# One written order for every operation, casting loads of GpSimd, and seven products from batch 2 on, in a fused attention and MLP kernel

## The chip, the cores and the metric

The kernel runs on one core of one Trainium2 chip. That core has five engines with a queue of instructions each: PE (TensorE, the matmuls), DVE (VectorE), ACT (ScalarE), POOL (GpSimd) and SP (SyncE, which here only issues DMAs), and 16 DMA engines that move data between HBM and SBUF. The metric is device time in microseconds: the median of several runs of the whole kernel. The kernel before takes **267.36 us** (median of 3 runs, 267.06 to 268.97).

## The reference

Two kernels are fused: an attention by landmarks (the Nystroem method), and behind it a layer norm with a two-layer MLP and a residual. There are 8 batches, 8 heads, 576 rows and 64 columns a head, so the MLP sees 8 x 576 rows of 512, with 2048 hidden columns.

```python
m, scale = 32, 1/sqrt(64)
q_lm, k_lm = means of 18 neighbouring rows of q and k      # 32 landmarks each
A  = softmax(scale * q    @ k_lm.T)      # 576 x 32
Bm = softmax(scale * q_lm @ k_lm.T)      # 32 x 32
C  = softmax(scale * q_lm @ k.T)         # 32 x 576
Z  = Bm.T / (norm1(Bm) * norminf(Bm) + 1e-06)
for _ in range(6):
    Z = 2 * Z - Z @ Bm @ Z               # towards the inverse of Bm
x  = A @ Z @ C @ v                       # heads side by side: 576 x 512 a batch
xn = (x - mean(x)) / sqrt(var(x) + 1e-06) * g_ln
out = x + relu(xn @ w_ch1) @ w_ch2       # w_ch1 512 x 2048, w_ch2 2048 x 512
```

Everything comes and goes as fp32. On the chip the matmuls take fp16.

## The kernel before, in words

**Stages of a batch.** The q, k and v of a batch come in six loads (two of each, four heads in one) of 128 partitions by 1152 fp32. Each lands in a staging tile (`stg`), from which another engine makes an fp16 copy: `nat` for q and k, `natv` for v. PE turns q and k (`TR`, L308), sums give the landmarks, small 32-wide matmuls do the six rounds on Z for all heads of a set of batches at once (sets are (1), (2), (3, 4), (5, 6), (7); batch 0 has its own code), and the products of exponentials (`ea`) with `m` give x, transposed for the MLP and in rows for the residual. The first layer of a batch is 16 chunks of 128 hidden columns, 16 matmuls' worth of K in four; its ReLU (`psh` to `hT`, fp16) is done by ACT or DVE. The second layer multiplies blocks of 128 rows of `hT` (4 blocks for an even batch, 5 for an odd one, which takes half a block along from the even one) with W2: 16 matmuls of 128x512 into one PSUM bank. DVE scales the bank by 1/std of the row and adds it to x (`xblk`), and the block is stored.

**Seven products.** From batch `FAST = 4` on, the first four blocks of a second layer (512 rows by 2048 by 512) are computed as a 2 x 2 by 2 x 2 product with seven products of quarter blocks instead of eight. Each of the seven is 16 matmuls of 128x256. The price is sums and differences of blocks: four mixes of W2 (`w2mix`, once for all batches, done by POOL in pieces of 128x512) and, for each batch, four mixes of hidden blocks in two pieces of 128x1024 each (`mix`, all on DVE), and 14 adds of 128x256 from PSUM into x instead of 4 of 128x512. The mixed blocks live in the ring of staging tiles.

**Weights.** W1 comes in 8 loads of 512 KB, is scaled by `g` on the way to fp16, and from batch 2 on is used in a form with its column mean taken away. W2 comes in 8 loads of 512 KB to staging tiles and is cast by POOL (`load_w2` L451, `cast_w2`). The instructions of the start stand in this order on their queues: batch 0's loads, W1's loads with POOL's scalings, four loads of batch 1 with their casts, then W2's loads with their casts, the last two loads of batch 1 among them.

```python
for i in range(8):
    if i == 3:
        for _ in range(2):
            b1.next_load()
            b1.next_cast()
    load_w2(i)
    cast_w2(i)
```

**What sets the order.** Every instruction on every engine is issued through `keep`, which fixes its place in the engine's queue; the place is chosen while the kernel is being built. A small planner (`Clock`) keeps for each engine an estimate of when it is free and for each tile of when it is written. Five streams of work (attention, totals, first layers, the first rows, second layers) offer their next operation with the time at which it could start, and the first that is ready by the estimate goes next; `help_out` puts loads, casts, mixes and stores between them when the engine they need is estimated to be free; a table (`AFTER`) holds some back until others have gone. Where nothing is ready, PE is given one matmul on zeros (`warm(1, 256)`, 20 such fillers with those of the start, of the form 128x256); and 27 matmuls of 128x160 on zeros stand ahead of everything. Tiles come from rings: a new one waits until the oldest of its ring has been read.

All loads and nearly all stores are issued by SP. All mixes of hidden blocks are on DVE. Casts of q and k are split: POOL 21, ACT 7, DVE 4 (32 loads).

Lines in the profile's rows: L298 is the helper through which DVE, ACT and POOL issue, L304 the matmuls, L308 the turns, L313 the loads of q, k and v, L451 those of W2.

Of the kernel before, what the change touches and what calls it, by code (L numbers as in the profile page):

```python
# [16 lines left out]
P = 128  # L17


@with_exitstack  # L20
def kernel(
# [16 lines left out]
    NGRP = NBLK // 4  # L38
# [10 lines left out]

    scale_qk = 1.0 / (D ** 0.5)  # L50
# [4 lines left out]
    nc.scalar.add_instruction(mybir.InstLoadActFuncSet(  # L55
        name=nc.get_next_instruction_name(), act_func_set_id=6, ins=[], outs=[]))

    const = ctx.enter_context(tc.tile_pool(name="const", bufs=1))
    wpool = ctx.enter_context(tc.tile_pool(name="wpool", bufs=1))


    NEVER = 1e12

    def name_of(x):
        return x.tensor.name if hasattr(x, "tensor") else x.name

    parted, mixed_, parted_w1 = {}, set(), set()

    def key_of(ap):

        return keys_of(ap)[0]

    def keys_of(ap):
        n = name_of(ap)
        if n not in parted:
            return [n]
        at = [ap.offset]
        for step, k in list(ap.ap)[1:]:
            if step >= parted[n]:
                at = [o + step * i for o in at for i in range(k)]  # L80
        if n in mixed_:
            return [f"{n}:{o // parted[n]}:{int(o % parted[n] >= 256)}" for o in at]
        return [f"{n}:{o // parted[n]}" for o in at]

    class Clock:


        WAY = 55.0
        OVERLAP = {"Activation": 110, "DVE": 80, "Pool": 30}

        def __init__(self):
            self.free = dict.fromkeys(("PE", "DVE", "Activation", "Pool", "SP"), 0.0)
            self.wrote, self.used, self.begun = {}, {}, {}
            self.small, self.lanes, self.wire = False, {}, 0.0
            self.cells, self.count, self.mark, self.fetched, self.ahead = [], 0, 95, 0.0, 0.0
            self.loads, self.pool = [], []
            self.free['PE'], self.issued = 1500.0, 0

        def share(self, span=3400.0):

            now = self.now()
            return sum(c for t, c in self.cells if t > now - span) / span

        def now(self):
            return max([self.free["PE"]] + list(self.lanes.values()))

        BLOCK, LEAD = 128, 16

        def both(self, *at):
            return max(max(at), ps2.next("p2", 2))  # L110

        def calm(self, n):

            return self.fetched if self.count + n + (20 if late() else 0) >= self.mark else 0.0

        def at(self, *tiles):
            return max([self.wrote.get(name_of(t), (0.0, ""))[0] for t in tiles] + [0.0]) + self.WAY

        def at_key(self, ap):
            return self.wrote.get(key_of(ap), (0.0, ""))[0] + self.WAY  # L120

        def idle_key(self, ap):
            n = key_of(ap)
            return max(self.wrote.get(n, (0.0, ''))[0], self.used.get(n, (0.0, ''))[0]) + self.WAY

        def idle(self, *tiles):

            return max([max(self.wrote.get(n, (0.0, ""))[0], self.used.get(n, (0.0, ""))[0],
                            self.begun.get(n, 0.0)) for n in map(name_of, tiles)] + [0.0]) + self.WAY

        def took(self, i, e, n, m):
            op = type(i).__name__
            if e == "Activation":
                return 300 if n < 8 else 190 + (1.07 if name_of(i.outs[0].bass_ap).startswith("ec_") else 0.79) * n
            if e == "Pool":
                if n == 1024 and name_of(i.outs[0].bass_ap) in mixed_:
                    return 2080
                if "Ptr" in op:
                    return 100 + 1.29 * n
                return 100 + 0.92 * n if "Copy" in op else 280 + 1.76 * n  # L140
            if n == 1152 and "Copy" in op:
                return 760
            if "Stats" in op:
                return 690 if m > 100 else 180
            if n >= 512 and (n == 576 or op == 'InstTensorCopy'):
                return 100 + 1.13 * n
            if n == 1024:
                last = max([b for a, b in self.pool if a <= self.ready < b] + [0.0])
                queued = 1000 if self.free["Pool"] > self.ready else 690
                return max(queued, last - self.ready + 560)  # L150
            if n == 256 and "Ptr" in op and name_of(i.outs[0].bass_ap).startswith("xblk"):
                return 480
            if "Transpose" in op:
                return 110 + 1.15 * n
            return 140 + 1.15 * max(n, m if "Reduce" in op else 0)

        def note(self, i):
            e = str(i.engine).rsplit(".", 1)[-1]
            outs = [a.bass_ap for a in i.outs if hasattr(a, "bass_ap")]
            ins = [a.bass_ap for a in i.ins if hasattr(a, "bass_ap")]  # L160
            size = [[k for _, k in a.ap] for a in outs + ins]
            count = []
            for dims in size:
                n = 1
                for k in dims[1:]:
                    n *= k
                count.append(n)
            reads = [n for a in ins for n in keys_of(a)]
            writes = [n for a in outs for n in keys_of(a)]
            ready = 0.0  # L170
            for n in reads:
                t, who = self.wrote.get(n, (0.0, e))
                if who != e or e != "PE":
                    ready = max(ready, t + (self.WAY if who != e else 0.0))
            for n in writes:
                for t, who in (self.wrote.get(n, (0.0, e)), self.used.get(n, (0.0, e)),
                               (self.begun.get(n, 0.0), "")):
                    if who != e:
                        ready = max(ready, t + self.WAY)
            if type(i).__name__ == "InstDMACopy":  # L180
                start = max(self.free[e], ready)
                self.free[e] = start + (580 if e == "SP" else 100)
                half_ = size[0][0] == 64 and any(n.startswith("stg") for n in writes)
                self.wire = (max(start + 1650, self.wire)
                             + count[0] * size[0][0] * 4 / (150.0 if half_ else 385.0))
                self.loads = self.loads[-24:] + [(start, self.wire)]
                self.issued += 1
# [3 lines left out]
            elif e == "PE":  # L191
                cols = count[0]
                if self.count == self.mark - self.LEAD:
                    self.ahead = self.now()
# [1603 lines left out]
```

## Time and profile before

| | before |
|---|---|
| median of the runs | 267.36 us (267.06 to 268.97) |
| span of the profiled execution, first to last instruction | 266.1 us |
| PE busy | 256.5 us, 96%, 3442 matmuls |
| DVE busy | 202.8 us, 76% |
| ACT busy | 175.2 us, 66% |
| POOL busy | 133.6 us, 50% |
| TensorE clock granted, mean | 0.999 |
| DMA moved | 46.68 MB, mean 175 GB/s |

The profiled execution is one run apart from the three that give the median; its span is 1.2 us below that median. "Busy" is the time in which an engine runs an instruction; the waits in between are named by what ended them. A group of rows in the list of costly instructions has the line, engine, operation, output and inputs, the shapes, the count, then the sum and the mean of one, then the idle time ahead of them by cause.

### The profile page before, as it was taken

To read this page: it belongs to the slowest core of one execution; us is meant where nothing else is said; L and a number is where in the kernel's file an instruction comes from. 1 tells how busy PE (TensorE), PEld (TensorE's weight loads), DVE (VectorE), ACT (ScalarE), POOL (GpSimd) and SP (SyncE) were. 2 spreads that over 40 slices of the span, in tenths; PEclk is the share of its full clock that TensorE was granted. 3 is DMA by queue.
4 is the path that set the end of the run, shared out by engine and by line. 5 is a ranking of instruction groups with operands and counts; after the bars stand their busy time and mean duration, and the time that the engine had idled before them with its cause. 6 is when DMAs were issued, how large, how long until landed. Compare 5 with 4: busy or idle time off the path is not lost.

```text
span 266.1 us, 8332 instructions
## 1 busy us (share of the span) xinstructions
PE 256.5 (96%) x3442; PEld 167.9 (63%) x3442; DVE 202.8 (76%) x461; ACT 175.2 (66%) x337; POOL 133.6 (50%) x160
## 2 busy tenths in 40 slices
PE   7889998999999999999999999999999999999994
PEld 7644754466545554546655465578878765788883
DVE  2657873899999979788984986989684599819762
ACT  2578997378868896589797559787377654871000
POOL 5288788999729387499999934500000042000000
PEclk9999999999999999999999999999999999999999
DMA  7999999999976996766611120110060006100606
GB/s 253 380 396 389 388 386 393 317 343 306 354 237 172 388 363 187 207 174 198 200 43 39 34 52 2 42 43 0 2 158 0 2 4 160 43 0 2 158 17 183
DMA packets 23566, 46.68 MB, mean 175 GB/s; under 512 B 2404, under 2 KB 2664, under 8 KB 23528
## 3 DMA queue, kind: packets, MB, share of 16 engines
q1 hardware_dynamic: 23048, 45.49, 53.3%
q10 hardware_dynamic: 480, 0.66, 0.7%
q8 instruction: 27, 0.44, 0.7%
q14 instruction: 11, 0.09, 0.1%
HBM read 36.70 MB, written 9.44 MB: 173 GB/s over the span
## 4 chain that ended last, share of the span: by engine, by line
PE 78%; DMA 11%; DVE 3%; POOL 3%; issue 2%; SPq 1%; ACT 1%; POOLq 0%; DVEq 0%
PE bank L304 51%; PE psh L304 21%; DMA stg<-in_v_dram 6%; DMA wstg<-in_moe_w_ch_dram 3%; DMA stg<-in_q_dram 2%; PE pscv L304 1%; POOL natv L298 1%; PE psd L304 1%; DVE xblk L298 1%; PE psec L304 1%; PE psm L304 1%; PE psea L304 1%; POOL w L298 1%; SPq L313 1%; DVE st L298 1%
## 5 line engine op out<-in xcount | busy, mean ns | idle before, releaser
L304 PE MATMUL bank<-w,hT 128*128 128x512 f16 (+3 forms) x528 | 111.7, 335 | 1.2 <-issue 0.8
L298 ACT ACTIVATE hT<-psh 128x576 f16<-128x576 f32 x119 | 73.6, 654 | 21.9 <-PE psh L304 21.0
L304 PEld LDWEIGHTS <-hT 128*128 128x128 f16 x656 | 60.3, 98 | 32.5 <-issue 8.6
L304 PE MATMUL psh<-ea,m 128*128 128x288 f16 x512 | 78.3, 286 | 0.6 <-DVE ea L298 0.3
L304 PEld LDWEIGHTS <-m 128*128 128x128 f16 x512 | 48.8, 97 | 20.2 <-issue 3.7
L298 DVE SCALAR_TENSOR_TENSOR xblk<-bank,rstd,xblk 128x256 f32<-128x256 f32 (+2 forms) x77 | 39.0, 539 | 22.4 <-PE bank L304 22.3
L298 POOL TENSOR_TENSOR ea<-ea,lns 128x576 f16<-128x576 f16 x14 | 18.9, 1371 | 60.4 <-ACT lns L298 54.6
L298 POOL CAST nat<-stg 128x1152 f16<-128x1152 f32 x21 | 23.8, 1147 | 8.5 <-DVE xT L298 6.4
L298 DVE BATCH_NORM_STATS2 six<-xblk 128x6 f32<-128x512 f32 x36 | 24.2, 673 | 0.9 <-ACT xblk L298 0.9
L298 POOL CAST natv<-stg 128x1152 f16<-128x1152 f32 (+1 forms) x17 | 19.3, 1165 | 9.7 <-DMA stg<-in_v_dram 7.7
L298 DVE STREAM_TRANSPOSE xT<-nat 128x576 uint32<-128x576 uint32 x28 | 21.4, 763 | 0.0
L298 ACT COPY xblk<-bank 128x512 f32<-128x512 f32 (+1 forms) x32 | 18.0, 591 | 4.0 <-PE bank L304 3.7
L304 PE MATMUL bank<-w2mix 128*128 128x256 f16 x128 | 17.1, 273 | 0.0
L304 PE MATMUL bank<-w2mix,hT 128*128 128x256 f16 x128 | 15.8, 273 | 0.0
L298 DVE SCALAR_TENSOR_TENSOR st<-st,bank 128x128 f16<-128x128 f16 (+2 forms) x36 | 11.1, 308 | 5.9 <-PE bank L304 5.7
L298 ACT CAST m<-bank 128x512 f16<-128x512 f32 x18 | 9.9, 586 | 7.5 <-PE bank L304 7.4
L298 DVE TENSOR_REDUCE part<-xT 128x32 f16<-128x576 f16 x20 | 14.6, 744 | 0.2
L298 ACT ACTIVATE lns<-psd 128x576 f32<-128x576 f32 x16 | 10.3, 644 | 6.0 <-PE psd L304 5.9
L304 PE MATMUL bank<-zcbd,ea 128*128 128x256 f16 x80 | 14.1, 273 | 0.0
L298 DVE SCALAR_TENSOR_TENSOR m<-less,zsum,bank 128x512 f16<-128x512 f16 (+1 forms) x18 | 11.5, 682 | 3.0 <-PE bank L304 1.4
L304 PEld LDWEIGHTS <-w2mix 128*128 128x128 f16 x128 | 12.4, 98 | 2.0 <-issue 0.2
L304 PEld LDWEIGHTS <-st 32*32 32x32 f16 x448 | 5.9, 90 | 11.9 <-DVE st L298 8.9
(135 smaller groups left out, 365.9 us busy)
## 6 DMA issues: line engine op xcount, KB each, us to landing
stg<-in_q_dram SPq DMA_DIRECT2D x16, 576.0 KB, 6.3
stg<-in_k_dram SPq DMA_DIRECT2D x16, 576.0 KB, 6.0
out_dram<-xblk SPq DMA_DIRECT2D x66, 128.0 KB, 2.4
wstg<-in_moe_w_ch_dram SPq DMA_DIRECT2D x16, 512.0 KB, 7.3
stg<-in_v_dram SPq DMA_DIRECT2D x10, 576.0 KB, 7.2
stg<-in_v_dram SPq DMA_DIRECT2D x6, 288.0 KB, 6.2
stg<-in_v_dram SPq DMA_DIRECT2D x12, 144.0 KB, 6.0
out_dram<-xblk ACTq DMA_DIRECT2D x4, 128.0 KB, 3.2
```

Of the source, the lines that this page charges most:

```text
L298: return lambda *args, **kw: keep(getattr(self.engine, op)(*args, **kw))
L304: keep(nc.tensor.matmul(o, l, r, start=start, stop=stop, tile_position=(rb, cb), skip_group_check=(skip or cb != 0)))
L313: keep(queue.dma_start(out=t[:], in_=src[b, 4 * u:4 * u + 4].rearrange("(r e) (t j) d -> (e t) r j d", e=2, j=NJ)))
```

## The change

The planner goes. Every operation gets a name and a list of engines that may do it, and one string of 1585 entries gives the order in which all operations are issued, and the engine of each:

```diff
+ORDER = """
+0G 1S 11D 10P 15P 16A 2S 236G 12D 18P 3S 13G 17P 4S 21P 23P 27D 19A 14A 20P 26P 28D 29P 30A 51P 52A
...
+    names = list(OPS)
+    order = [(names[int(x[:-1])], x[-1]) for x in ORDER.split()] if ORDER else [(n, OPS[n][0][0]) for n in names]
+    for n, e in order:
+        emit(n, e)
```

`emit` takes a free buffer of the right kind for each tile that the operation is the first to use, and frees it after its last use, so buffers are no longer rings. The stages of a batch, the sets and the arithmetic of each stage stay.

W2 comes in four DMAs of 128x4x512 that GpSimd issues straight into the fp16 tile (the DMA casts); in the order the first of them stands behind the loads of q and k of batch 1, the other three behind those of batch 2 and behind GpSimd's two casts of v of batch 1.

```diff
-    def load_w2(i):
-        stg = stage.tile([P, 2, DM], FP32, name="wstg", tag="stg")
-        keep(nc.sync.dma_start(out=stg[:], in_=w2_src[:, ts(i, 2), :]))
-        w2_coming.append(stg)
-    def cast_w2(i):
-        pool.tensor_copy(out=w2_16[:, ts(i, 2), :], in_=w2_coming[i][:])
+        for i in range(4):
+            op(f"load_w2_{i}", "G", (),
+               lambda e, i=i: dma(e, w2_16[:, ts(i, 4), :], w2_src[:, ts(i, 4), :]))
```

q and k of batches 1 to 7 come likewise, in 14 DMAs of GpSimd into fp16 tiles with both halves of a batch in one (1.18 MB of fp32 read each). Batch 0's q and k, and all v, still come as fp32 and are cast by an engine.

The seven products start two batches earlier, and a mix of hidden blocks may go to GpSimd:

```diff
-    FAST = 4
+    FAST = 2
...
-    def mix(o, left, right, op, k):
-        n = ds(k, 4)
-        dve.tensor_tensor(out=o[:, n, :], in0=left[:, n, :], in1=right[:, n, :], op=op)
+                def mix(e, i=i, c=c):
+                    o, x, y = mixes[i][1]()
+                    tt(e, o[:, ds(c, 4), :], x[:, ds(c, 4), :], y[:, ds(c, 4), :], mixes[i][2])
+                op(f"hmix_{b}{i}{c}", "DG", uses, mix)
```

In the new order, 33 of the 48 mixes of hidden blocks are GpSimd's, 11 ReLUs go from ACT to DVE, some casts of v go from GpSimd to DVE and ACT, and 20 whole stores instead of 4 are issued by ACT. The fillers are gone but for the 27 matmuls at the very start:

```diff
-                if at[k] > now + 250 and clock.share() < 0.5 and banks.next() <= now:
-                    warm(1, 256)
-                    continue
...
-        if (w, nm) != (U - 1, "k"):
-            warm(3, 256)
```

More of the change, by code (lines that the diff above doesn't have):

```diff
@@ L1422 @@
+    HK, HN = MCH // 2, DM // 2
     w11, w12 = w2_16[:, 0:HK, 0:HN], w2_16[:, 0:HK, HN:DM]
     w21, w22 = w2_16[:, HK:MCH, 0:HN], w2_16[:, HK:MCH, HN:DM]
[L1425 to L1438 removed]
```

2330 lines of the change are left out of this document (908 added, 1422 removed), and 9 rows, old and new, of the table AFTER.

## The prediction

> **What bounds the kernel now.** I read the page's head first (who is busy, the clock, the chain that ended last), then four stretches of the span, then what TensorE itself waits for.
>
> ```profile
> span 266.1 us, 8332 instructions
> ...
> PE 256.5 (96%) x3442; PEld 167.9 (63%) x3442; DVE 202.8 (76%) x461; ACT 175.2 (66%) x337; POOL 133.6 (50%) x160
> ...
> PEclk9999999999999999999999999999999999999999
> ...
> PE 78%; DMA 11%; DVE 3%; POOL 3%; issue 2%; SPq 1%; ACT 1%; POOLq 0%; DVEq 0%
> ```
>
> ```profile
> 0.00:50.00 50.00, 45.11 (x706) 28.50 (x707) 31.12 (x89) 32.87 (x62) 36.40 (x61) 1.00 1.00 371
> 50.00:100.00 50.00, 50.00 (x635) 28.77 (x634) 46.46 (x100) 41.16 (x79) 37.20 (x42) 1.00 0.93 305
> 100.00:160.00 60.00, 59.09 (x943) 33.23 (x941) 49.55 (x110) 44.05 (x90) 48.93 (x51) 1.00 0.45 125
> 160.00:240.00 80.00, 79.76 (x960) 58.04 (x958) 58.69 (x130) 56.46 (x106) 11.02 (x8) 1.00 0.16 38
> ```
>
> ```profile
> PE bank L304 <- DVE zeros L340: 1.5, 1, 1.5
> ...
> PE bank L304 <- issue: 0.8, 1, 0.8
> PE bank L304 <- POOL w L298: 0.5, 1, 0.5
> ```
>
> The columns of the stretches are length, then busy time of PE, weight loads, DVE, ACT, POOL, then clock, DMA share, GB/s. Two kernels stand in one span. Up to 50 us the DMA engines are full (share 1.00 at 371 GB/s) and PE is idle for 50.00 - 45.11 = 4.9 us. From 50 to 240 us PE is idle for 0.00 + 0.91 + 0.24 = 1.15 us of 190. So behind the start almost nothing is left to win from a better order: the time falls by what PE no longer has to compute, or by an earlier start. Two more things are read from these rows: DVE is at 46.46 of 50 in the second stretch, and POOL is nearly idle (11.02 of 80) in the fourth.
>
> **The change part by part.** Counts of instructions are those of the two programs.
>
> *Seven products for batches 2 and 3.* Their eight blocks of 16 matmuls 128x512 become two times seven products of 16 matmuls 128x256.
>
> ```profile
> 99.61 1.47 PE L304 MATMUL bank<-w,hT 128*128 128x512 f16 x6
> 100.92 0.65 PE L304 MATMUL psh<-ea,m 128*128 128x288 f16 x4
> 101.41 0.22 PE L304 MATMUL bank<-st,bones 128*128 128x128 f16 x1
> ...
> 188.25 1.91 PE L304 MATMUL bank<-w2mix,hT 128*128 128x256 f16 x16
> 190.00 1.91 PE L304 MATMUL bank<-w,hT 128*128 128x256 f16 x16
> ```
>
> From start to start (a mean duration overlaps its neighbour), six wide matmuls take 100.92 - 99.61 = 1.31 us, 0.218 each; a whole product takes 1.75. Per batch: 64 x 0.218 = 13.95 before, 7 x 1.75 = 12.25 after. Two batches: **-3.4 us**, on the path, as PE has no idle time there. All other matmuls keep their number and form, but for 20 fillers (below).
>
> *What the seven products add on DVE and POOL.* The mixes of hidden blocks go from 32, all on DVE, to 48: 15 on DVE and 33 on POOL. The adds of 128x256 go from 56 to 84, those of 128x512 from 19 to 11.
>
> ```profile
> L298 POOL CAST nat<-stg 128x1152 f16<-128x1152 f32 x21 | 23.8, 1147 | 8.5 <-DVE xT L298 6.4 <-DMA stg<-in_k_dram 1.1 <-PE bank L304 0.4
> L298 POOL TENSOR_TENSOR w2mix<-w 128x512 f16<-128x512 f16 x8 | 9.0, 1151 | 0.0
> L298 POOL CAST w<-wstg 128x1024 f16<-128x1024 f32 x8 | 8.1, 1038 | 1.2 <-DMA wstg<-in_moe_w_ch_dram 0.7 <-PE psd L304 0.3
> ...
> L298 DVE SCALAR_TENSOR_TENSOR xblk<-bank,rstd,xblk 128x256 f32<-128x256 f32 x56 | 24.2, 476 | 20.4 <-PE bank L304 20.3
> L298 DVE SCALAR_TENSOR_TENSOR xblk<-bank,rstd,xblk 128x512 f32<-128x512 f32 x19 | 13.8, 731 | 0.0
> L298 DVE TENSOR_SCALAR hT<-psh 128x576 f16<-128x576 f32 x9 | 6.8, 754 | 1.0 <-PE psh L304 0.8
> L298 DVE TENSOR_TENSOR w2mix<-w2mix,hT 128x1024 f16<-128x1024 f16 x8 | 6.3, 792 | 0.0
> L298 DVE TENSOR_TENSOR hT<-hT 128x1024 f16<-128x1024 f16 x8 | 5.2, 683 | 0.0
> ...
> L298 ACT CAST nat<-stg 128x1152 f16<-128x1152 f32 x7 | 8.0, 1159 | 0.0
> ```
>
> No row shows POOL on a two-input mix of 1024. It lies between the 1.04 of a one-input cast of that size and twice the 1.15 of a mix of 512, 2.3; I take 2.1, near the double, because the mix is the same operation: 33 x 2.1 = 69 us of POOL. DVE: 17 mixes fewer at about 0.73 (-12.4), 28 adds of 0.476 more (+13.3), 8 adds of 0.731 fewer (-5.8), 11 relus taken from ACT (9 become 20; 11 x 0.754 = +8.3), and about 12 of small things (5 casts of v, copies of m, mixes of W2, scalings of W1). 202.8 + 15 = about **218 us**, 82% of the span instead of 76. ACT loses the 11 relus and 7 casts (8.0): about 160. All this is cover, not path, as long as PE never waits for it; what it costs if it does is the second rival.
>
> *Casting DMAs.* POOL loses 20 casts of q and k (22.9), the 8 of W2 (8.1) and about 18 us of casts of v, scalings and other operations given to DVE and ACT; it gains 18 DMA issues (14 of 1.18 MB for q and k, 4 of 1.05 MB for W2). The trace has no DMA issued by POOL. The nearest rows are SP's issue of a load half as large and what POOL does when it touches every element:
>
> ```profile
> 0.80 0.44 SPq L313 DMA_DIRECT2D stg<-in_q_dram  x1
> ...
> 37.38 2.36 POOL L298 CAST natv<-stg 64x1152 f16<-64x1152 f32 x2 [0.40 <-DMA stg<-in_v_dram]
> 39.80 3.99 POOL L298 CAST w<-wstg 128x1024 f16<-128x1024 f32 x4
> 44.08 1.04 POOL L298 CAST w<-wstg 128x1024 f16<-128x1024 f32 x1 [0.28 <-PE psd L304]
> ```
>
> One issue costs between 0.44 and 2.3 us (two casts of 1.15, its own share of elements); I take 0.9, two issues of SP, since it is an issue. 18 x 0.9 = 16. POOL then holds 133.6 - 49 + 69 + 16 = about **170 us** (bounds: 127 to 202), with the new mixes where the fourth stretch has it idle. Off the path in the sum.
>
> *The start.* It is DMA-bound, so bytes in order set it.
>
> ```profile
> stg<-in_q_dram SPq DMA_DIRECT2D x16, 576.0 KB, 6.3
> ...
> wstg<-in_moe_w_ch_dram SPq DMA_DIRECT2D x16, 512.0 KB, 7.3
> ```
>
> A batch's q, k and v are six loads of 0.59 MB, a weight eight of 0.52. Ahead of the last quarter of W2 the old order has 3.5 MB (batch 0), 4.2 (W1), 3.5 (batch 1) and W2's own 4.2, 15.5 MB: 41.7 us at 371 GB/s, and the trace has W2's last cast at 44.08 to 45.1. The new order puts q and k of batch 2 (2.36 MB) ahead, and the last three quarters of W2 stand on POOL's queue behind both casts of batch 1's v: 17.8 MB, 48 us, landing near 50. So W2 is complete about 5 us later. What covers it: 13 of batch 0's 16 first-layer chunks now stand ahead of its first second-layer matmul instead of 8, 5 chunks of 101.41 - 100.92 = 0.49, 2.5 us; left +2.5. Against it: POOL, which cast q, k, v and W2 one after another up to 45 us, is rid of 12 of these (12.8 us), and PE's 4.9 us of idle time there have something to shrink. I set -2.5 for that and **0** for the start, with ends of +7 (no cover) and -8 (all idle time and the fillers gone).
>
> *Fillers.* 20 matmuls on zeros go, 17 of them in five groups from the first to the last of these rows.
>
> ```profile
> L304 PE MATMUL bank<-zeros 128*128 128x256 f16 x20 | 3.3, 274 | 0.0
> ```
>
> ```profile
> 6.62 0.49 PE L304 MATMUL bank<-zeros 128*128 128x256 f16 x3
> ...
> 13.50 0.61 PE L304 MATMUL bank<-zeros 128*128 128x256 f16 x4
> ```
>
> They stand where PE would wait, so they are worth 0 in the sum; what kept warm by them is the third rival.
>
> *Order.* Of the 1.15 us of idle time behind 50 us I take half: **-0.6**. The stores go partly to ACT's queue (20 instead of 4 whole ones, 16 x 0.44 = 7 us of issuing on an engine at 66%): nothing. The SP queue loses 36 loads, and a load now waits behind fewer stores: nothing.
>
> The sum against the profiled execution: 266.1 - 3.4 + 0 - 0.6 = 262.1. The runs' median, 267.36, lies 1.2 over the span; so **263.3 us**, 1.5% faster.
>
> **Rivals.**
>
> *W2 late (slower).* Place: the first 50 us, where the DMA share is 1.00 and nothing is spare. Of the 17.8 MB, 8.9 are now cast on the way. If casting halves the rate of these bytes, they take 8.9 / 0.371 = 24 us more of the DMA engines; half of that lies beside first-layer work and batch 1's attention, 12 us do not: 266.1 - 3.4 + 12 - 0.6 + 1.2 = 275 us. It decides as soon as W2's last quarter lands after about 53 us. For it: W2 comes last, and its issue waits in POOL's queue behind casts that wait for v. Against: a casting load reads the same bytes and writes half.
>
> *DVE becomes the bound (no change).* DVE is at 93% in the second stretch already and gets 15 us more. If 3 to 5 us of it fall where PE waits for a bank, the gain is gone: 266.1 - 3.4 + 3.5 + 1.2 = 267.4. [...]
>
> *The clock (no change).* The clock was granted in full (1.00) in all stretches. Without fillers the front of batch 0 has gaps.
>
> ```profile
> L308 PE MATMUL pst<-ident,nat 128*128 128x128 f16 x36 | 3.1, 242 | 0.9 <-DVE nat L298 0.8
> ...
> L304 PE MATMUL bank<-pm,nat 128*128 128x64 f16 x36 | 1.7, 194 | 0.2 <-DVE nat L298 0.2
> ```
>
> At half the clock these would take twice as long: 266.1 - 3.4 - 0.6 + 4.8 + 1.2 = 268.1. [...]
>
> *A better start (faster still).* Half of the start's 8.2 us (4.9 idle, 3.3 fillers) goes: 266.1 - 3.4 - 0.6 - 4.1 + 1.2 = 259.2.
>
> **How the numbers follow.** The forecast 0.36 (its own range 260.5 to 264.6), the better start 0.14, DVE 0.26, the clock 0.05, W2 late 0.19. 1% of 267.36 is 2.7 us, about what a measurement of this kernel tells from no change; faster is below 264.7: 0.36 + 0.14 = 0.50. Within 1%: 0.26 + 0.05 = 0.31. Slower: 0.19. The range 257 to 271 takes in the first four cases and the light end of the last; what it leaves out is most of W2 late and the best of starts.
>
> **What would show it.** The seven products: 672 matmuls 128x256 of them at 1.75 us a product, and none of the wide ones in batches 2 and 3 but the fifth block's. The start: PE's idle time in 0 to 50 us (4.9 before), and the landing of the last W2 load (50 forecast). POOL: the mix of 1024 at 2.1 us, the issue at 0.9. DVE: busy 218, its mixes near 0.73 rather than over 1, and no wait of PE for DVE above 1 us in all behind 50 us. The clock: digits of 9 throughout. The forecast is wrong if PE's idle time behind 50 us rises above 4 us, or if PE is past 50 us with less done than before: the start is the term I know least.

## The result

The changed kernel takes **281.37 us** (median of 6 runs, 279.54 to 282.27) against 268.06 for the kernel before in the same runs: a ratio, estimated from the single runs, of 1.0479 (95% interval 1.042 to 1.0538). It is **4.8% slower**; forecast was 263.3, with a range of 257 to 271. Here and below, medians take in all runs, and ratios leave out the few that fell into a slower state of the chip.

### The profile after

The page's head, as it was read of the kernel before; the profiled execution is the fastest of the six, its span 11.7 us longer than the one before.

```profile
span 277.8 us, 8397 instructions
...
PE 256.3 (92%) x3518; PEld 179.6 (65%) x3518; DVE 221.4 (80%) x491; ACT 165.1 (59%) x316; POOL 169.3 (61%) x167
...
PEclk9956999999999999998999999999999999999997
...
PE 72%; DVE 17%; ACT 3%; DMA 2%; issue 2%; SPq 0%; ACTq 0%
```

Then the same four stretches (length, busy PE, weight loads, DVE, ACT, POOL, clock, DMA share, GB/s).

```profile
0.00:50.00 50.00, 41.68 (x664) 26.69 (x665) 34.34 (x94) 32.74 (x58) 30.13 (x60) 0.90 1.08 276
50.00:100.00 50.00, 46.71 (x560) 26.10 (x558) 47.96 (x95) 29.48 (x61) 31.48 (x34) 1.00 0.75 164
100.00:160.00 60.00, 57.07 (x1071) 41.37 (x1070) 55.89 (x125) 44.39 (x89) 49.36 (x45) 0.97 0.57 125
160.00:240.00 80.00, 79.06 (x937) 58.95 (x935) 59.74 (x129) 50.26 (x94) 42.98 (x24) 1.00 0.20 48
```

The engines' sums are as forecast: DVE 221 (218 forecast), POOL 169 (170), ACT 165 (160). What was not: PE is idle for 8.3 us up to 50 us (4.9 before) and for 3.29 + 2.93 + 0.94 = 7.2 us from 50 to 240 (1.15 before). DVE's share of the chain that ended last went from 3% to 17%. The clock's row has a 5 and a 6 near the start and an 8 in the middle. The two longest waits of PE behind the start (sum, times, longest):

```profile
PE it L192 <- DVE st L209: 3.1, 3, 2.3
PE psea L192 <- ACT lns L202: 2.5, 1, 2.5
```

To place the loss, TensorE's **useful work** is added up along the trace: each matmul on data counts with the time from its start to the next one's, but at most with the pace of its form where nothing waits, the median distance of two starts in the trace of the changed kernel (0.109 us for 256 columns, 0.123 for 288, 0.216 for 512; for the small tiles 0.06 is taken, where those of 128x128 start 0.056 apart). What is missing against the kernel before at the same moment is time lost so far.

| useful work done, us | by 20 | by 40 | by 60 | by 90 | by 120 | by 130 | by 190 | in all |
|---|---|---|---|---|---|---|---|---|
| before | 7.1 | 24.4 | 40.8 | 67.4 | 93.5 | 102.8 | 157.7 | 225.4 |
| changed | 5.9 | 18.9 | 36.8 | 60.4 | 87.2 | 92.4 | 145.3 | 223.1 |
| missing | 1.2 | 5.5 | 4.0 | 7.0 | 6.3 | 10.4 | 12.4 | |

So there is a loss at the start (5.5, of which 4.0 stay), one of 3.0 between 60 and 90 us and one of 4.1 between 120 and 130. Against it stand 2.3 us less work, the seven products. The last matmul is 9.2 us later than before, which leaves 0.4 net for the stretches in between. What is still missing lies behind it: the last operation of DVE ends 262.97 before and 272.20 now, the spans end 3.1 and 5.6 us later, 2.4 more. 4.0 + 3.0 + 4.1 + 0.4 - 2.3 + 2.4 = 11.6 of the 11.7.

The middle first. DVE, POOL, ACT and PE about 120 us (start, duration, and in brackets the idle time ahead and what ended it):

```profile
118.34 0.78 POOL L222 DMA_DIRECT2D nat_q<-in_q_dram  x1
118.55 4.44 DVE L206 TENSOR_TENSOR ea<-ea,lns 128x576 f16<-128x576 f16 x1
119.14 2.13 POOL L206 TENSOR_TENSOR hT<-hT 128x1024 f16<-128x1024 f16 x1
121.21 1.17 POOL L199 CAST natv<-stg_v 128x1152 f16<-128x1152 f32 x1
122.32 0.95 POOL L206 TENSOR_TENSOR s_q<-asum_q,nat_q 128x128 f16<-128x128 f32 x1
...
123.08 0.65 ACT L202 ACTIVATE lns<-psd 128x576 f32<-128x576 f32 x1 [3.56 <-DVE ea L206]
123.79 0.43 PE L192 MATMUL psea<-xT_q,lmt_k 32*32 32x288 f16 x20 [2.49 <-ACT lns L202]
```

One operation of DVE on operands in SBUF took 4.44 us; another of its form in this run took 0.75. POOL ran all that time with no gap between its instructions, and DVE was done 0.6 us after the third of them. No gap opened for it there either: POOL's fourth instruction, the sum `s_q`, began at once and took 0.95 us, where the ten of its form take 0.50 on average. ACT waited for DVE's result, PE for ACT's. The clock records then show half speed from 124.2 to 127.6 us. Between 60 and 90 us two more stand out:

```profile
64.00 0.78 POOL L222 DMA_DIRECT2D nat_q<-in_q_dram  x1 [1.40 <-DVE xT_k L219]
64.19 2.07 DVE L206 TENSOR_TENSOR mix<-w 128x512 f16<-128x512 f16 x1
64.80 1.17 POOL L206 TENSOR_TENSOR mix<-w 128x512 f16<-128x512 f16 x1
...
74.47 3.16 DVE L206 TENSOR_TENSOR w<-w,less 128x1024 f16<-128x1024 f16 x1
74.82 1.14 POOL L206 TENSOR_TENSOR mix<-w 128x512 f16<-128x512 f16 x1
75.93 1.15 POOL L206 TENSOR_TENSOR asum_q<-nat_q 128x512 f32<-128x512 f16 x1
77.16 1.06 POOL L206 TENSOR_TENSOR asum_q<-asum_q 128x256 f32<-128x256 f32 x1
...
80.67 0.24 PE L192 MATMUL it<-st 32*32 32x64 f16 x8 [2.31 <-DVE st L209]
```

The mix of 64.19 takes 2.07; the same form took 0.38 at 52.47 us. PE waits 0.9 us for what DVE does behind it. The operation of 74.47, which centres W1, ends at 77.63, just behind the first gap in POOL's row (77.08 to 77.16); its form takes 0.67 elsewhere. What DVE had to do behind it, a cast of v of 1.29 us among it, came late, and PE's rounds on Z waited 2.3 us.

The casting loads did what was forecast. Two rows of queues (packets, MB written, share of the 16 DMA engines' time in the span): that of the casting loads after the change, and that of the loads and stores before:

```profile
q0 software_dynamic: 9504, 10.36, 23.6%
```

```profile
q1 hardware_dynamic: 23048, 45.49, 53.3%
```

The row of the casting loads counts 10.36 MB written, which are 20.7 MB read as fp32: 23.6 / 20.7 = 1.14% per MB read, against 53.3 / 45.49 = 1.17% before. So the GB/s of the stretches (276 against 371) fall because half as much is written, not because the loads are slower. W2's last quarter landed at 50.0 us, the forecast's 50, and no wait of PE is for a DMA.

### The profile page after: what moved, and what is told of

Same layout as the page of the kernel before. It is cut to its first block, busy times and chain, and to the rows that moved or that the text cites. A ratio compares the mean times of both kernels' runs of the same rounds, so it can differ in the third digit from the quotient of the medians.

```text
span 277.8 us, 8397 instructions
## 1 busy us (share of the span) xinstructions
PE 256.3 (92%) x3518; PEld 179.6 (65%) x3518; DVE 221.4 (80%) x491; ACT 165.1 (59%) x316; POOL 169.3 (61%) x167
## 3 DMA queue, kind: packets, MB, share of 16 engines
q0 software_dynamic: 9504, 10.36, 23.6%
## 4 chain that ended last, share of the span: by engine, by line
PE 72%; DVE 17%; ACT 3%; DMA 2%; issue 2%; SPq 0%; ACTq 0%
PE psh L192 20%; PE ps7a L192 14%; PE pso L192 9%; PE ps7c L192 8%; PE ps7e L192 3%; PE psy L192 3%; PE psm L192 3%; PE it L192 3%; DMA stg_k<-in_k_dram 2%; DVE m L209 2%; PE pscv L192 2%; DVE m L199 2%; DVE ea L206 2%; DVE w L206 2%; PE psf L192 1%
## 5 line engine op out<-in xcount | busy, mean ns | idle before, releaser
L192 PEld LDWEIGHTS <-m 128*128 128x128 f16 x512 | 47.5, 98 | 20.7 <-issue 3.9
L192 PE MATMUL pso<-w,hT 128*128 128x512 f16 x176 | 44.1, 380 | 0.1
L206 POOL TENSOR_TENSOR mix<-hT 128x1024 f16<-128x1024 f16 x7 | 14.9, 2125 | 30.6 <-ACT hT L202 20.0
L206 POOL TENSOR_TENSOR ea<-ea,lns 128x576 f16<-128x576 f16 (+1 forms) x14 | 16.7, 1193 | 24.5 <-ACT lns L202 15.4
L209 DVE SCALAR_TENSOR_TENSOR x<-ps7a,rstd,x 128x256 f32<-128x256 f32 x48 | 21.4, 473 | 6.7 <-PE ps7a L192 6.5
L192 PE MATMUL ps7a<-mix,hT 128*128 128x256 f16 x192 | 25.7, 276 | 0.0
L206 POOL TENSOR_TENSOR mix<-mix,hT 128x1024 f16<-128x1024 f16 x10 | 21.5, 2156 | 6.3 <-DVE mix L206 5.9
L934 DVE BATCH_NORM_STATS2 six<-x 128x6 f32<-128x512 f32 x36 | 24.2, 672 | 0.0
L206 POOL TENSOR_TENSOR hT<-hT,mix 128x1024 f16<-128x1024 f16 x9 | 19.0, 2121 | 6.9 <-PE ps7e L192 6.9
L199 ACT CAST m<-psm 128x512 f16<-128x512 f32 x31 | 17.1, 592 | 9.7 <-PE psm L192 7.1
L1003 DVE TENSOR_SCALAR hT<-psh 128x576 f16<-128x576 f32 x20 | 14.9, 750 | 9.2 <-PE psh L192 8.9
L192 PEld LDWEIGHTS <-mix 128*128 128x128 f16 x192 | 18.6, 99 | 3.5 <-issue 0.6
L199 ACT COPY x<-psy 128x512 f32<-128x512 f32 (+1 forms) x33 | 19.2, 586 | 2.2 <-PE psy L192 1.8
L202 ACT ACTIVATE lns<-psd 128x576 f32<-128x576 f32 x16 | 10.4, 650 | 12.0 <-PE psd L192 6.6
## 6 DMA issues: line engine op xcount, KB each, us to landing
w1s<-in_moe_w_ch_dram SPq DMA_DIRECT2D x8, 512.0 KB, 11.6
```

Source lines behind the costliest of these rows:

```text
L192: keep(nc.tensor.matmul(o, l, r, start=start, stop=stop, tile_position=(rb, cb), skip_group_check=(skip or cb != 0)))
L199: keep(nc.scalar.copy(o, i) if e == "A" else ENGINES[e].tensor_copy(out=o, in_=i))
L202: keep(nc.scalar.activation(*args, **kw))
L206: keep(ENGINES[e].tensor_tensor(out=o, in0=a, in1=b, op=f))
L209: keep(ENGINES[e].scalar_tensor_tensor(out=o, in0=a, scalar=s, in1=b, op0=f0, op1=f1))
L934: keep(nc.vector.bn_stats(out=T(f"six_{j}")[:], in_=T(f"x_{j}")[:]))
```

## The experiments

All times are medians; the ratios are to the kernel before on the same chip.

| run | median, us | ratio, 95% interval | span |
|---|---|---|---|
| changed kernel | 281.37 | 1.0479 (1.042 to 1.0538) | 277.8 |
| fill | 281.80 | 1.0500 (1.0468 to 1.0532) | 280.1 |
| unblock | 275.82 | 1.0268 (1.0223 to 1.0313) | 274.2 |
| one_ea | 277.94 | 1.0373 (1.0293 to 1.0453) | 274.3 |
| tail | 278.12 | 1.0368 (1.0334 to 1.0402) | 276.9 |
| allthree (fill, unblock, tail) | 272.96 | 1.0194 (1.0135 to 1.0254) | 271.4 |
| two_edits (unblock, tail) | 273.43 | 1.0207 (1.0159 to 1.0255) | 271.0 |
| mixes_on_dve | 298.42 | 1.1120 (1.1066 to 1.1174) | 294.5 |
| eight_in_2_3 | 287.00 | 1.0727 (1.0666 to 1.0787) | 284.8 |
| start | 283.74 | 1.0600 (1.0568 to 1.0632) | 281.8 |
| start2 | 283.01 | 1.0532 (1.0475 to 1.0589) | 279.4 |
| start3 | 279.50 | 1.0433 (1.0390 to 1.0476) | 276.9 |
| before_no_fillers | 269.99 | 1.0089 (1.0059 to 1.0119) | 268.8 |
| before_five | 271.91 | 1.0129 (1.0088 to 1.0170) | 269.5 |
| before_b1_first | 279.79 | 1.0419 (1.0366 to 1.0472) | 278.3 |
| before_b1_both | 285.15 | 1.0647 (1.0611 to 1.0683) | 283.3 |

### The clock at the start: fill, two_edits, before_no_fillers

Run fill, the changed kernel with matmuls on zeros put back:

```diff
+    def fillers(i, n):
+        def go(e):
+            t = pools["bank"].tile([P, 512], FP32, name="idle", tag=f"bank{free['bank'][-1]}")
+            for _ in range(n):
+                MM(t[:, 0:256], zeros[:, 0:P], zeros[:, 0:256])
+        op(f"filler_{i}", "P", (), go)
+    for i, n in enumerate((4, 6, 1, 2, 4, 5, 2, 2, 3, 4, 3)):
+        fillers(i, n)
```

> The changed kernel with 36 matmuls 128x256 on zeros put back between batch 0's first operations (11 places, 3 to 16 us). Theory A (the lost start is the halved clock from 15.0 to 25.2 us, set off by TensorE's gaps before it): the clock stays at 1.00, the 8.5 us of busy time in that stretch shrink by about 4, and the span falls from 277.8 to 273 to 274.5. Rival (TensorE is late there because of the order of the operations and of the loads, and the slow clock only stretches waits): the clock recovers, the span falls by less than 1.5 us.

Measured: 281.80 us, no gain. The stretch from 10 to 20 us, and the next, first of the changed kernel, then of fill:

```profile
10.00:20.00 10.00, 7.07 (x133) 5.07 (x131) 6.55 (x20) 3.99 (x8) 2.45 (x3) 0.75 1.07 306
20.00:30.00 10.00, 8.40 (x156) 4.54 (x155) 7.05 (x18) 8.64 (x17) 5.09 (x8) 0.74 1.08 327
```

```profile
10.00:20.00 10.00, 8.22 (x166) 5.67 (x164) 5.92 (x20) 4.62 (x7) 2.02 (x3) 1.00 1.09 325
20.00:30.00 10.00, 7.94 (x172) 4.75 (x170) 7.55 (x19) 8.64 (x17) 4.69 (x7) 1.00 1.03 286
```

The clock is back at 1.00, and the useful work by 40 us is 18.5, not more than the 18.9 without fillers. Theory A is refuted: the clock does fall at the start, but bringing it back wins nothing there. The pair of allthree and two_edits, with and without the fillers, says the same (272.96 and 273.43; the latter at a clock of 0.55 from 10 to 20 us):

> The run with the three edits together, without its 36 fillers. If the clock that falls at the start without them costs nothing, because the steps there wait for each other and not for TensorE's speed: within 1.5 us of 272.96. If the halved clock costs what TensorE's busy time in it says: 275.5 or more.

In the kernel before, where PE has more to do at that time, taking the fillers away does cost:

```diff
         idle = banks.take([P, 512])
+        if cols == 256:
+            clock.free["PE"] = clock.now() + 110 * n
+            return
```

> The kernel before without its 20 fillers of 128x256 (the 27 matmuls at the very start stay). If gaps alone halve the clock at the start and this costs time: a stretch at 0.5 of 3.4 to 10.2 us within the first 30, and 2 to 5 us more. If the clock falls but the small dependent steps there don't wait for TensorE's speed, as the run with fillers suggests: less than 1.5 us more.

Measured: 2.2 us more, with 3.4 us at half clock from 15.9. So that is what the fillers were worth in the kernel before, where the forecast had them at 0; the changed kernel's start hangs on something else.

### DVE held off by POOL: unblock, one_ea, mixes_on_dve

In unblock five entries of the order change; 731 is the scaling of ea at 118.55, 578 the mix of hidden blocks beside it, 492 the centring at 74.47, 438 a cast of v, and 500 a mix of W2:

```diff
-500D
+500G
...
-492D
-438D
+438A
...
+492D
 493D
...
 1375G
-578G
 588D
...
 730A
+731G
+578G
 732P
...
 1043A
-731D
 1044S
```

> The changed kernel with four operations moved or given to another engine: the scaling of ea that took 4.44 us on DVE at 118.6 goes to POOL ahead of the mix beside it, the mix of W2 that took 2.07 on DVE at 64.2 goes to POOL, the centring of W1 that took 3.16 at 74.5 goes behind the rounds on Z, and one cast of v from DVE to ACT. Theory B (a DVE operation with only SBUF operands waits for a gap in a run of POOL instructions): TensorE's waits of 2.5 us at 121 and 2.3 at 78 go, and with the first the halved clock of 124.2 to 127.6 (1.7 us): the span falls by 5 to 6.5 us. Rival (DVE is simply full, the wait moves to the next DVE operation): it falls by less than 2.5.

This text takes the mix of W2 that was moved for the one of 64.19, but it is another: entry 500 is the mix that DVE did in 0.38 us at 52.47. The long one stayed on DVE and is as long in unblock:

```profile
66.21 2.07 DVE L206 TENSOR_TENSOR mix<-w 128x512 f16<-128x512 f16 x1
```

Measured: 275.82 us, **5.6 less**. PE's waits of 2.5 and 2.3 us are gone and the clock stays at 1.00 behind the start; the 0.9 us behind the long mix are still there. Counted as useful work, 2.1 us are won between 60 and 90 us and 3.6 between 90 and 130. The first part comes from two moves at once, the centring put behind the rounds on Z and the cast of v given to ACT; how much of it is owed to POOL and how much to the order alone was not separated. To see how much the one operation at 118.55 is worth, one_ea has only the moves of 731 and 578:

> The changed kernel with one operation moved: the scaling of ea that took 4.44 us on DVE at 118.6 goes to POOL, ahead of the mix of hidden blocks beside it. If DVE was held off by POOL's run of instructions: TensorE's wait of 2.5 us at 121 and the halved clock of 124.2 to 127.6 go, 3.5 to 4.5 us of the 5.5 that the four moves brought together. If DVE's load is the cause: less than 1.5.

Measured: 277.94 us, 3.4 less, just short of the 3.5 expected (2.8 less by the ratios; the runs lie between 276.0 and 281.1). The span is 3.5 shorter. Two stretches, first of the changed kernel, then of one_ea:

```profile
118.00:124.00 6.00, 3.51 (x77) 2.57 (x76) 6.00 (x6) 2.41 (x4) 5.25 (x5) 1.00 0.69 96
124.00:130.00 6.00, 6.00 (x136) 3.96 (x105) 4.93 (x13) 2.90 (x6) 5.16 (x4) 0.72 0.58 160
```

```profile
118.00:124.00 6.00, 6.00 (x152) 4.63 (x149) 4.88 (x12) 4.33 (x7) 5.98 (x6) 1.00 0.69 105
124.00:130.00 6.00, 5.96 (x70) 4.25 (x61) 5.75 (x12) 4.50 (x8) 6.00 (x6) 1.00 0.95 299
```

POOL is busier than before (11.98 of these 12 us, 10.41 before). DVE issues 24 operations instead of 19 in about the same busy time (10.63 us, 10.93 before), and PE has hardly any idle time: it was the meeting of one DVE operation with a run of POOL instructions, not DVE's load. Theory B holds for this operation, but for its gap: no gap in POOL's row let DVE go on. The opposite cure, all mixes back on DVE, shows what POOL's share was good for:

```diff
-575G 577G 576G
+575D 577D 576D
...
```

> The changed kernel with all 48 mixes of hidden blocks on DVE, one letter each in the order. DVE gets 33 x 0.69 = 23 us and loses the stretches that a busy POOL sets off. Theory B (DVE is held off by runs of POOL instructions): no DVE operation over 2.5 us is left behind 100 us, the wait of 2.5 us at 121 goes, and the span falls by 1 to 4 us. Rival (DVE's own amount of work is the bound): the span rises by 3 us or more.

Measured: 298.42 us, 17 more; the rival is right here. The meeting is gone, as theory B has it: the same scaling of ea, now at 123.25 us, takes 0.74. But PE's longest waits (sum, times, longest) are now for DVE's own work:

```profile
PE ps7a L192 <- DVE x L209: 5.2, 3, 3.6
PE it L192 <- DVE st L209: 3.5, 4, 2.3
```

### The end: tail, and the three together

In tail, batch 6's last two adds (1368, 1365) and its stores go ahead of batch 7's:

```diff
 1508D
+1368D
+1365D
+1359A
+1360S
+1357A
+1366S
+1369A
+1367S
+1370A
 1520D
```

> The changed kernel with the last two adds of batch 6 put ahead of batch 7's on DVE, and batch 6's stores ahead of batch 7's on the queues. Theory C (5.6 us pass behind the last matmul, 3.1 before, because the last stores queue behind others): the span falls by 1.5 to 2.5 us. Rival (the stores' landing takes that long anyway): less than 0.8.

Measured: 278.12 us, 3.2 less in the median. The store queue of SP, and DVE's last operation, first of the changed kernel, then of tail:

```profile
266.58 7.75 SPq L222 DMA_DIRECT2D out_dram<-x  x9
...
271.85 0.35 DVE L209 SCALAR_TENSOR_TENSOR x<-pso_74b,rstd,x 128x128 f32<-128x128 f32 x1 [0.28 <-PE pso_74b L192]
```

```profile
268.73 5.25 SPq L222 DMA_DIRECT2D out_dram<-x  x6
```

```profile
273.07 0.35 DVE L209 SCALAR_TENSOR_TENSOR x<-pso_74b,rstd,x 128x128 f32<-128x128 f32 x1 [0.28 <-PE pso_74b L192]
```

Behind DVE's last operation lie 276.9 - 273.42 = 3.5 us instead of 5.6: three stores less stood ahead of the last one. Theory C holds for these 2.1 us. DVE's last operation comes 1.2 later in the profiled run of tail, the slowest of its four, so that the two profiled spans differ by only 0.9; the 3.2 of the medians, more than the 1.5 to 2.5 expected, has an interval wide enough for 2.1.

> The edits of the three other runs together. If A, B and C hold and add up: 277.8 - 4 - 6 - 2 = 266 for the span, 267 to 270 as a median, the time of the kernel before. If the lost time only moves to other waits: 273 or more.

Measured: 272.96 us, 8.4 less: the 5.6 of unblock and the 3.2 of tail add up, fill adds nothing. So the time misses the 267 to 270 that were expected if all three theories held, by about the 4 us set down for theory A. The stretches of allthree:

```profile
0.00:50.00 50.00, 43.30 (x700) 28.11 (x701) 34.47 (x94) 32.55 (x58) 29.74 (x60) 1.00 1.05 270
50.00:100.00 50.00, 48.58 (x578) 27.40 (x577) 47.32 (x99) 32.18 (x66) 34.04 (x36) 1.00 0.83 176
100.00:160.00 60.00, 59.56 (x1136) 43.46 (x1133) 55.14 (x132) 46.52 (x92) 54.65 (x48) 1.00 0.53 121
160.00:240.00 80.00, 79.06 (x913) 59.51 (x912) 58.50 (x125) 48.95 (x91) 42.91 (x24) 1.00 0.20 50
```

From 50 to 240 us PE is idle for 2.8 us instead of 7.2, in spite of DVE at 215 and POOL at 171 us in all. What is left against the kernel before is the start: 18.6 of useful work by 40 us.

### What the seven products are worth: eight_in_2_3, before_five

> The run with the three edits together, with batches 2 and 3 again as blocks of eight products: 64 matmuls 128x512 each in the places of the seven products, no mixes of hidden blocks and 4 adds instead of 14 in each. If the seven products gain what they save on TensorE: 3 to 3.5 us slower than 271.4. If that gain is eaten by waits for DVE and POOL: within 1 us, or faster.

In it FAST is 4 again, and the blocks of batches 2 and 3 stand where their products stood. Measured: 287.00 us, 14 more. TensorE's useful work rises from 222.8 to 225.4, 2.6 us where 3 to 3.5 were expected (some matmuls are missing in the records), but PE is also idle for 8.9 of the 90 us from 100 to 190 (1.0 in allthree), waiting for DVE in the rounds on Z. The written order was not made for blocks there; the run doesn't price the seven products, and why the waits are so long stays open. The kernel before with its planner is the better place for that question:

```diff
-    HK, HN, FAST = MCH // 2, DM // 2, 4
+    HK, HN, FAST = MCH // 2, DM // 2, 5
```

> The kernel before with seven products from batch 5 on instead of 4: one batch less. If seven products gain what they save on TensorE, 13.95 - 12.25 = 1.7 us a batch: 1.2 to 2.2 us slower than before. If the gain is eaten by the mixes and adds on DVE: within 0.7 us.

Measured: a ratio of 1.0129, 2.4 to 4.5 us, where 1.2 to 2.2 were expected. Useful work rises from 225.4 to 227.1, the 1.7 of the forecast; the rest is idle time of PE that the planner's new order brought (78.66 busy of the 80 us from 160 to 240, 79.76 before) and a few small waits. In the kernel before, seven products gain what they save on TensorE.

### The start: before_b1_first, before_b1_both, start, start2, start3

The first chunk of batch 0's first layer, in the kernel before and after (the latter row gives the first and the last start in its window):

```profile
21.09 0.41 PE L304 MATMUL psh<-ea,m 128*128 128x288 f16 x2
```

```profile
L192 PE MATMUL psh<-ea,m x12: 286/286/297, 30.9 to 32.8; 128*128 128x288 f16 x12
```

It comes 10 us later; the eighth load of W1 landed at 24.1 us before and at 29.1 now. In the changed order q of batch 1 (1.18 MB) is issued ahead of seven of W1's loads, k ahead of the last four. The same was done to the kernel before:

```diff
+    b1 = sets[0]
     for i in range(8):
+        if i == 2:
+            b1.next_load()
+            b1.next_load()
+        if i == 6:
+            b1.next_cast()
+            b1.next_cast()
         load_w1(i)
...
-    b1 = sets[0]
-    for _ in range(4):
+    for _ in range(2):
         b1.next_load()
         b1.next_cast()
```

> The kernel before with the two loads of k of batch 1 put ahead of the last six loads of W1 instead of behind all eight, as the changed kernel has a load of q of batch 1 there. If the bytes ahead of W1 set the start: 1.18 MB at 371 GB/s, 3.2 us more. If W1's later quarters have slack: within 1 us.

In this run, by 40 us 21.2 of useful work are done instead of 24.4, 3.2 less, the size of 1.18 MB at 371 GB/s. The time rises by 12 us, far more than the 3.2 expected: by 50 us 4.4 are missing, and the planner's estimates and its table, made for the other order, lose the rest later. In before_b1_both the two loads of q follow at `i == 6`:

> The kernel before with both loads of k of batch 1 ahead of the last six loads of W1 and both of q ahead of the last two: the bytes of batch 1 stand about where the changed kernel has them. Counted is TensorE's useful work done by 40 us, 24.4 us' worth before, 21.2 with k alone ahead, 18.9 in the changed kernel. If what stands ahead of W1 sets the start: 18 to 20. If the order of the changed kernel's small operations does: 21 or more.

Measured: 16.9 by 40 us, a little more lost than expected and more than the changed kernel loses (18.9); 285.15 us in all. The rows from 20 to 30 and from 30 to 40 us, of the kernel before, with k ahead, and with both ahead:

```profile
20.00:30.00 10.00, 9.48 (x94) 5.48 (x87) 7.84 (x17) 8.80 (x17) 7.99 (x9) 1.00 1.05 389
30.00:40.00 10.00, 10.00 (x142) 6.83 (x139) 8.16 (x23) 8.80 (x23) 7.95 (x8) 1.00 1.05 387
```

```profile
20.00:30.00 10.00, 7.46 (x57) 4.15 (x50) 6.47 (x14) 5.79 (x11) 8.72 (x11) 0.83 0.89 294
30.00:40.00 10.00, 10.00 (x142) 6.74 (x141) 7.35 (x16) 8.57 (x20) 5.41 (x5) 1.00 1.03 380
```

```profile
20.00:30.00 10.00, 7.66 (x57) 4.19 (x57) 6.47 (x15) 5.82 (x10) 6.71 (x8) 0.83 0.82 300
30.00:40.00 10.00, 7.15 (x66) 4.56 (x65) 2.90 (x6) 4.44 (x10) 7.37 (x9) 0.83 0.94 318
```

With loads of batch 1 ahead of W1, most engines get less to do from 20 us on, and the losses of 3.2 and 7.5 us by 40 us are of the size of the changed kernel's 5.5. But bytes are not all that differs: the casts of batch 1 move too, and the DMA engines are not full (0.89 and 0.82 from 20 to 30 us), since in both runs SP issues no load from 18.3 to 22.8 us while it waits. The clock falls as well, to 0.83.

The trace of the changed kernel also has another candidate, the order of small operations. The first scaling of W1, before and after:

```profile
14.38 1.36 POOL L298 TENSOR_SCALAR w<-wstg,g_sb 128x512 f16<-128x512 f32 x2 [0.50 <-DVE st L298]
```

```profile
18.67 0.97 POOL L355 TENSOR_SCALAR w<-w1s,g_sb 128x512 f16<-128x512 f32 x1 [2.96 <-DVE g_sb L1136]
```

POOL waits 3 us for `g`, the factors of the scaling, which PE turns at 17.0 us now and at 11.4 before; the first of W1 had landed at 14.9. SP waits 8.5 us, until 19.7, for a staging tile that a scaling frees, and only then issues the fifth load of W1 (at 12.5 before). PE's last product of batch 0's rounds on Z begins at 25.0 us, 18.4 before, and the chain of work that ended last has no DMA between 9.1 and 45 us. The casting loads kept the DMA engines full meanwhile (1.07 from 10 to 20 us), so earlier loads of W1 would have pushed others back; the trace alone doesn't settle which of the two counts.

The test from the other side, W1 ahead again in the changed kernel, gave no gain in three orders. Run start rewrites the first 150 entries (by hand, from the kernel before):

> The run with the three edits together, and its first 150 entries rewritten in the manner of the kernel before: both halves of batch 0 turned and cast (by DVE) at once, W1's loads in order with q and k of batch 1 behind six of them instead of ahead of five, its scaling mostly on POOL again, and batch 0's first chunks ahead of batch 1's preparation; 20 fillers at other places. Theory D (the start is lost by order: the first chunk of the first layer begins at about 30 us, 21 before, with nothing of equal size brought forward): the first chunk comes at 22 to 25 us and the span falls from 271.4 to 266 to 268.5. Rival (the bytes of the casting loads set the start whatever the order): it stays within 1.5 us of 271.4.

> As the run with the rewritten start, which let batch 1's preparation stand ahead of the third and fourth quarter of batch 0's first layer and of W1's scaling; here three quarters of batch 0's first layer (10 of 16 chunks) stand ahead of it, as in the kernel before. Theory D (the start is lost by order): 10 chunks are begun by about 32 us (before: 11; the changed kernel: none), the span falls from 271.4 to 266 to 269. Rival (with the casting loads of batch 1 behind W1 its preparation comes late instead, and the time is lost there): 272 or more.

> The run with the three edits together, with small moves in its start alone: batch 1's early loads and preparation stay where they are; W1's second load comes second, the scaling of W1's first quarter goes from ACT to POOL (idle there for 4 us), k of the second half of batch 0 is copied ahead on ACT, v is cast by POOL, the last round on Z isn't held behind other products, and the mean and the first two chunks of the first quarter stand ahead of the second quarter and of the copies of x. Theory D' (W1's late arrival and the order behind it hold back batch 0's first chunk, 30.6 us): the first chunk comes at 24 to 27 us, and of 5.8 us of work missing at 40 us against the kernel before 2 to 4 come back: span 267.5 to 269.5. Rival (what is moved ahead holds back batch 1's preparation by as much): 270.5 to 273.

Measured: 283.74, 283.01 and 279.50 us, all slower than the 272.96 that they began from. None reaches the gain that its theory set down, and start3 lies above its rival's range too. In the first two the first chunk comes at 24.2 us, as expected, but batch 1's preparation then stands still; by 60 us 26.8 and 27.7 of useful work are done (36.3 in allthree). In start2 POOL shows why (sum, times, longest):

```profile
POOL nat_k L223 <- PE psl_k L193: 12.3, 1, 12.3
```

A casting load of batch 2 waits 12.3 us in POOL's queue for its buffer, and the casts of v and three quarters of W2 wait behind it. In start3 the first chunk doesn't move (30.6 us), and one of the new losses is the one known from the middle:

```profile
15.84 0.80 POOL L223 DMA_DIRECT2D nat_k<-in_k_dram  x1
...
16.44 1.69 DVE L207 TENSOR_TENSOR ea<-ea,lns 128x288 f16<-128x288 f16 x1
16.64 2.51 POOL L200 CAST natv<-stg_v 128x1152 f16<-128x1152 f32 x2
```

DVE's scaling of ea, 0.45 us in the changed kernel, meets the issue of a casting load and two casts of v that were moved to POOL, and takes 1.69. So it is shown that loads of batch 1 ahead of W1 cost the start of the kernel before 3.2 and 7.5 us. How much of the changed kernel's loss there they are, and how much is the order of the small operations, stays open, since no order with W1 first and everything else in place was found. No version here beats the kernel before.

## Why the prediction was wrong, step by step

The time lies 10 us above the range, and both signs that the prediction named for being wrong came true: PE's idle time from 50 to 240 us is 7.2 us (4 was the limit behind 50 us), and about 50 us less work is done than before (5.5 us are missing by 40, 4.0 by 60).

**Seven products, -3.4 us: right in mechanism.** Useful work falls by 2.3 us in the records (the few matmuls missing in a trace limit that), one batch's by 1.7 in before_five, as forecast.

**"All this is cover, not path, as long as PE never waits for it": the step that failed first.** The sums were sized well: a mix of 1024 on POOL takes 2.12 to 2.16 us (2.1 forecast), an issue of a casting load 0.75 to 1.04 (0.9), POOL's and DVE's busy times came out within 2%. But a sum of busy time doesn't say whether two instructions meet. The rival of DVE becoming the bound was weighed by its load, with 3.5 us of waits for it. That term was the author's estimate, and no run shows it; what the trace shows in its place are seven operations of DVE, all with operands in SBUF alone and each with POOL at work beside it, that took over 0.4 us longer than their form does elsewhere, about 10 us in all, and three of them are 7.9 of these. The longest, with the halved clock that it brought, cost 3.4 us (one_ea); the centring of W1, together with what stood beside it, 2.2 more (unblock); the mix of W2 was never moved, and PE's wait of 0.9 us behind it stayed. In the longest, DVE was held through several POOL instructions in a row: 4.44 us instead of 0.75, beside a DMA issue, a mix and a cast. The kernel before had the like on a small scale: of its 32 mixes of hidden blocks three took 0.97, 1.10 and 1.57 us, at 163.6, 165.1 and 217.2 us, each beside a scaling of `ea` on POOL, and the other 29 took 0.68. The forecast weighed a sum, and a single long meeting decided.

**The start, 0: wrong, though inside its ends.** The working asked when W2 lands, found 50 us, and that was exact, and no wait came from it. The same rule of bytes in order was not applied to W1: q and k of batch 1 had moved ahead of most of it, 2.36 MB or 6.4 us at 371 GB/s, and the first layer of batch 0 needs W1 well before the second layer needs W2. Nor did the working ask when batch 0's small operations would run: `g` is turned 5.6 us later, the last product of the rounds on Z begins 6.6 us later. That 4.0 to 5.5 us were lost there is measured; how they divide between these two stays open. The rival of a late W2 had the right sign and 8 of the 13 us (275), but by luck: its own condition, W2 landing after 53 us, wasn't met, and the halved rate of casting loads isn't there (1.14% of the DMA engines' time per MB read, 1.17% per MB before).

**Fillers, 0, and the clock.** The clock fell at the start as the rival feared (half speed for 10.2 us, from 15.0 to 25.2), and matmuls did start twice as far apart there (those of 128x128 by 0.107 us instead of 0.056). But no run shows the price of 4.8 us: with the clock back at 1.00, fill takes 281.80 us against 281.37, and two_edits, at 0.55 from 10 to 20 us, 273.43 against 272.96. The 20 fillers of the kernel before were worth 2.2 us there (before_no_fillers), not 0. In the changed kernel a fall stood beside a loss in the middle, behind a wait that the forecast didn't have. In its clock records the fall behind the wait at 121 lasts 3.4 us, the one at the start 10.2, three times as much. The same wait of 2.3 us at 78 was followed by a fall in fill (81.3 to 84.7) and by none in the changed kernel; what decides between the two is not shown.

**Order, -0.6, and stores at nothing: wrong.** PE's idle time from 50 to 240 us went up by 6 us, and the stores, counted as nothing because they moved to a less busy queue, cost 2.4 us at the end. What stood ahead of the last store were adds and stores of batch 6; without them 2.1 of the 2.4 come back (tail).

**The chances.** Slower had 0.19, and all of it on one mechanism. Held-off operations, a later start of the first layer and a longer tail were each small, and all pointed the same way.

## What to carry to other kernels

Moving work to an idle engine is priced by the instructions it will run beside, not by its busy time alone: look for the operations of DVE on SBUF operands that the path hangs on, and keep runs of POOL instructions away from them (4.44 us instead of 0.75 here), or give them to POOL, as one_ea did (3.4 us less). At a start bound by transfers (DMA share 1.00 up to 50 us in the kernel before), check every weight in the order of its use, not just the last to land, and the small operations that free its staging tiles. A load issued by a computing engine waits for its buffer in that engine's queue, with everything behind it (12.3 us in start2). At the end, see what stands ahead of the last store (2.1 us in tail).

## What the runs showed of the hardware

- A DVE operation on SBUF operands (a scaling of `ea`, a mix of W2, the centring of W1) was held through up to three POOL instructions in a row: 4.44 us instead of 0.75, 2.07 instead of 0.38, 3.16 instead of 0.67. Once it ended just behind a gap of 0.08 us in POOL's row (77.08 to 77.16); at 118.55 it ended with no gap there, while POOL's next instruction took 0.95 us instead of 0.50. What lets it go on is open. The issue of a casting load on POOL seems to be part of such a run (64.00 and 118.34).
- A load that casts fp32 to fp16 took the DMA engines as long for each byte read as one that doesn't (1.14% of their time per MB read in the queue of the casting loads of the changed kernel, 1.17% per MB in the queue of loads and stores of the kernel before).
- Behind a wait of PE of 2.3 to 2.5 us the clock was halved for 3.4 us (behind 121 us in the changed kernel, behind 78 in fill) or not at all (behind 78 in the changed kernel).
